# Scaling x by one bound per batch, and splitting and turning it by halves of the heads

## The chip, the core and the metric

The kernel runs on one core of one Trainium2 chip. The metric is the device time of one execution in microseconds; less is better. Before the change the median of three runs is 897.0 us (894.86, 897.0 and 897.5).

## What is computed

Attention in which a query sees only the keys of its own hash bucket, then a gated feed-forward layer ("MoE") on the result:

```python
q_bits = einsum('bhsd,dk->bhsk', q, proj) > 0      # 6 bits; k_bits likewise
mask = q_bucket[:, :, :, None] == k_bucket[:, :, None, :]
scores = where(mask, matmul(q, k.T) / sqrt(64), -1e9)
attn = softmax(scores)                             # sum + 1e-9
x = matmul(attn, v)                                # 4 batches, 8 heads, 768 tokens, 64
x = x.transpose(0, 2, 1, 3).reshape(3072, 512)
out = ((x @ w_a) * (x @ w_b)) @ w_out              # 512 -> 1536 -> 512
```

## The kernel before, in words

A *unit* is (b, c): one batch and 256 of its 768 tokens (b 0 to 3, c 0 to 2), 12 in all. It is handled in two *halves* of four heads, and a half is eight q-tiles of 128 queries by 768 keys. I call (b, c, half) a block.

For a q-tile TensorE makes the scores (L1053), VectorE the row maximum (L1067) and a width (L1076), ScalarE or VectorE a bias (L1083, L1089), and ScalarE the exponential with its row sum (L1099). The exponentials are split into a float16 hi part (L1110 to L1112) and the rest, lo (GpSimd L1122 or VectorE L1126), turned by a transposing DMA (L1132), and multiplied with the hi and lo parts of V in 18 matmuls (L1141, "av"). Unit (0,0) is done in float32 instead, and turned by TensorE (L1020, L1027, L1034). The products of a block collect in one PSUM tile `av`, of which there is one buffer.

V is loaded by pairs of heads; `vprep` (L765 on) takes a pair's largest value (`scale_pair`, L741 on: a reduction on ScalarE L751 or VectorE L754, then `scale_of`: a matmul, a maximum, three small instructions, L460 to L480), makes a power of two of it (`vsc`), and `veps`, a guard for the softmax sum (L780), and splits V into hi (L790, L794) and lo (L802). K and Q go through `split` (L883 to L904) and are turned by DMA, at the start by TensorE (L855) with an eviction (L863, L865).

`su_end` (L1149 on) closes a block. It makes r from the row sums (L1166, L1171, L1179), x = av * r (L1184), and for each token the sum of the absolute values of x (`sums`, L1195). After the second half `norm` (L1206 on) makes a power of two for each token with eight small instructions. Then x of the whole unit is scaled by it and split, one tile of 128 tokens after the other, into hi (L1237, L1241) and lo (L1248), each tile in two pieces, and each tile is turned by one DMA (L1260) into `xT`. In the first and the last unit x is scaled first (L1269), turned in float32 by TensorE (L1283) and split while it is evicted (L1295, L1298).

The MoE layer of a unit has 12 steps f. A step multiplies xT with two weights (L1346, 24 matmuls, tile `ab`), gates the two products (ScalarE L1360, VectorE L1368), splits the result (L1376 or L1380, GpSimd L1388), and multiplies with the output weight (L1398, tile `o`). At the end the scale is undone with `osc` (L1417), one column for each token tile, in the two evictions `ob` (L1428, L1434), and two DMAs store them (L1452). The tag `ob` has two buffers. The weights arrive as 64-bit numbers in the first quarter and are turned into hi and lo parts on all engines (L529 to L662).

The order of all work is fixed: each piece is an *entry* with a number, and the list `ORDER` names the entries in the order in which they are issued. Every engine runs its own entries in that order, and SP issues all DMAs in that order. Plus 10000 or 20000 picks an entry's first or second other engine. A negative number stands for that many filler matmuls on a dummy tile (`warm`, L1502). A tile takes a buffer of its tag when it is first written, and the buffer comes free when the last entry that uses the old tile is done.

Of the kernel before, what the change touches and what calls it, by code (L numbers as in the profile page):

```python
# [1540 lines left out]
```

## Time and profile before

| | |
|---|---|
| median of three runs | 897.0 us |
| profiled execution | 895.02 us, span 893.2 us |
| TensorE busy | 859.5 us, 9213 matmuls |
| VectorE busy | 649.4 us, 1561 instructions |
| ScalarE busy | 529.8 us |
| GpSimd busy | 450.8 us |
| TensorE's granted clock, mean | 0.998 |

The span runs from the first to the last instruction of the profiled execution. Busy times are of instructions at work; waiting for a semaphore is not busy. The filler matmuls count as busy TensorE time.

### The profile page before, as it was taken

To read this page: it belongs to the slowest core of one execution; us is meant where nothing else is said; L and a number is where in the kernel's file an instruction comes from. 1 tells how busy PE (TensorE), PEld (TensorE's weight loads), DVE (VectorE), ACT (ScalarE), POOL (GpSimd) and SP (SyncE) were. 2 spreads that over 40 slices of the span, in tenths; PEclk is the share of its full clock that TensorE was granted. 3 is DMA by queue.
4 is the path that set the end of the run, shared out by engine and by line. 5 is a ranking of instruction groups with operands and counts; after the bars stand their busy time and mean duration, and the time that the engine had idled before them with its cause. 6 is when DMAs were issued, how large, how long until landed. Compare 5 with 4: busy or idle time off the path is not lost.

```text
span 893.2 us, 23061 instructions
## 1 busy us (share of the span) xinstructions
PE 859.5 (96%) x9213; PEld 655.1 (73%) x9213; DVE 649.4 (73%) x1561; ACT 529.8 (59%) x1031; POOL 450.8 (50%) x396
## 2 busy tenths in 40 slices
PE   5789899999999999999999999999999999999998
PEld 4567777767777767777777777777777777777775
DVE  6899999888878968777875468777888865562210
ACT  7789999865654655566634466545675645442212
POOL 2578887663456465565153364554444455361111
PEclk9999999999999999999999999999999999999999
DMA  9986899999999999999977779997999957644000
GB/s 325 308 185 199 152 257 201 175 166 174 179 197 176 161 195 187 192 175 176 172 136 112 119 159 157 181 180 142 162 188 160 175 108 121 114 95 72 2 24 25
DMA packets 416988, 142.61 MB, mean 160 GB/s; under 512 B 388592, under 2 KB 409200, under 8 KB 416880
## 3 DMA queue, kind: packets, MB, share of 16 engines
q1 hardware_dynamic: 416880, 141.14, 82.4%
q8 instruction: 72, 1.18, 0.6%
q14 instruction: 36, 0.29, 0.1%
HBM read 37.82 MB, written 6.29 MB: 49 GB/s over the span
## 4 chain that ended last, share of the span: by engine, by line
PE 70%; DVE 6%; ACT 2%; DMA 2%; issue 1%; POOL 0%; ACTq 0%; SPq 0%; DVEq 0%
PE ab L1346 35%; PE o L1398 17%; PE s L1053 9%; PE av L1141 8%; DMA at<-a 2%; DVE mx L1067 1%; ACT e L1099 1%; DVE g L1368 1%; DVE xz L1248 1%; ACT a L1111 0%; DMA xT<-xz 0%; DVE a L1126 0%; DVE x L1184 0%; PE b_k L816 0%; PE b_q L816 0%
## 5 line engine op out<-in xcount | busy, mean ns | idle before, releaser
L1346 PE MATMUL ab<-xT,wab 128*128 128x256 f16 x3456 | 409.0, 273 | 2.2 <-DVE g L1368 1.9
L1346 PEld LDWEIGHTS <-wab 128*128 128x128 f16 x3456 | 332.3, 98 | 56.6 <-issue 4.1
L1122 POOL TENSOR_TENSOR a<-e,a 128x768 f16<-128x768 f32 x128 | 215.6, 1687 | 106.0 <-ACT a L1111 55.9
L1388 POOL TENSOR_TENSOR g<-g,g 128x256 f16<-128x256 f32 x144 | 106.2, 738 | 241.8 <-ACT g L1376 165.3
L1099 ACT ACTIVATE e<-s,bias,width 128x768 f32<-128x768 f32 x192 | 189.7, 988 | 62.3 <-DVE bias L1089 48.7
L1067 DVE TENSOR_REDUCE mx<-s 128x1 f32<-128x768 f32 x192 | 182.2, 951 | 43.7 <-PE s L1053 42.6
L1398 PE MATMUL o<-wo,g 128*128 128x512 f16 x864 | 208.3, 379 | 0.0
L1360 ACT ACTIVATE a<-ab,wcut 128x256 f32<-128x256 f32 x144 | 67.6, 469 | 136.8 <-PE ab L1346 135.7
L1368 DVE SCALAR_TENSOR_TENSOR g<-ab,wlow,a 128x256 f32<-128x256 f32 x132 | 63.5, 481 | 109.4 <-ACT a L1360 101.2
L1398 PEld LDWEIGHTS <-g 128*128 128x128 f16 x864 | 81.8, 98 | 75.9 <-issue 0.2
L1141 PEld LDWEIGHTS <-at 128*128 128x128 f16 x3168 | 112.3, 98 | 20.7 <-DMA at<-a 3.6
L1141 PE MATMUL av<-vh,at 128*128 128x64 f16 x2112 | 115.6, 193 | 2.3 <-DMA at<-a 1.7
L1053 PE MATMUL s<-kTA_k,qTA_q 128*128 128x384 f16 x384 | 94.5, 328 | 5.6 <-ACT e L1099 3.9
L1053 PE MATMUL s<-kTB_k,qTB_q 128*128 128x384 f16 x384 | 94.5, 328 | 0.0
L1112 POOL CAST a<-e 128x768 f16<-128x768 f32 x62 | 55.1, 893 | 41.5 <-ACT e L1099 31.5
L1083 ACT ACTIVATE bias<-mx,width 128x1 f32<-128x1 f32 x89 | 25.9, 293 | 73.0 <-DVE width L1076 72.9
L1111 ACT CAST a<-e 128x768 f16<-128x768 f32 x77 | 63.7, 829 | 7.8 <-DMA at<-a 6.7
L1376 ACT CAST g<-g 128x256 f16<-128x256 f32 x98 | 39.3, 401 | 44.7 <-DVE g L1368 37.5
L1141 PE MATMUL av<-vl,at 128*128 128x64 f16 x1056 | 59.6, 193 | 0.0
L1053 PEld LDWEIGHTS <-qTB_q 128*128 128x128 f16 x384 | 37.7, 98 | 25.3 <-issue 0.7
L1126 DVE TENSOR_TENSOR a<-e,a 128x768 f16<-128x768 f32 x48 | 47.4, 991 | 8.4 <-ACT a L1111 8.0
L1053 PEld LDWEIGHTS <-qTA_q 128*128 128x128 f16 x384 | 34.7, 99 | 22.5 <-issue 7.9
(156 smaller groups left out, 857.3 us busy)
## 6 DMA issues: line engine op xcount, KB each, us to landing
rk_k<-in_k_dram SPq DMA_DIRECT2D x16, 384.0 KB, 4.2
vr<-in_v_dram SPq DMA_DIRECT2D x16, 384.0 KB, 3.9
rq_q<-in_q_dram SPq DMA_DIRECT2D x12, 512.0 KB, 5.0
raw_w<-in_moe_w_b_dram SPq DMA_DIRECT2D x12, 512.0 KB, 7.6
raw_w<-in_moe_w_a_dram SPq DMA_DIRECT2D x12, 512.0 KB, 6.7
raw_wo<-in_moe_w_out_dram SPq DMA_DIRECT2D x12, 512.0 KB, 5.1
out_dram<-ob SPq DMA_DIRECT2D x24, 256.0 KB, 2.6
at<-a SPq DMA_TRANSPOSE x176, 4.1
```

Of the source, the lines that this page charges most:

```text
L1053: nc.tensor.matmul(ps.t[:, jj, :HALF], lhsT=x.t[:, uq, :], rhs=y.t[:, h * NT + jj * 3 : h * NT + jj * 3 + 3, :].rearrange("p t x -> p (t x)"),
L1067: lambda: nc.vector.tensor_reduce(out=mx.t[:, u : u + 1], in_=halves(ps.t), axis=AX.XY, op=ALU.max, negate=True),
L1099: lambda: nc.scalar.activation(flat2(e.t), halves(ps.t), AF.Exp, bias=bias.t[:, u : u + 1], scale=width.t[:, u : u + 1], accum_out=sm.t[:, ...
L1111: ("ACT", 0.725, lambda: nc.scalar.copy(out=a2.t[:, 0], in_=e.t), False),
L1112: ("POOL", 0.9, lambda: nc.gpsimd.tensor_copy(out=a2.t[:, 0], in_=e.t), False),
L1122: lambda: nc.gpsimd.tensor_tensor(out=a2.t[:, 1], in0=e.t, in1=a2.t[:, 0], op=ALU.subtract),
L1141: nc.tensor.matmul(av.t[:, u, :], lhsT=at.t[:, a + kt, :], rhs=w.t[:, h, kt, :], start=i == 0, stop=i == 3 * NT - 1,)
L1346: nc.tensor.matmul(pl.t[:, m, :CH], lhsT=wt(m, wi, cc, f), rhs=xt.t[:, :, xi * NC + cc, :], start=i == 0, stop=i == 3 * NC - 1,)
L1360: lambda a=a, pl=pl, gr=gr: nc.scalar.activation(a.t, pl.t[:, 0, :CH], AF.Copy, scale=wcut[:, gr : gr + 1]),
L1368: lambda a=a, g32=g32, pl=pl, cut=cut: nc.vector.scalar_tensor_tensor(out=g32.t, in0=pl.t[:, 1, :CH], scalar=cut, in1=a.t, op0=ALU.mult, o ...
L1388: lambda g=g, g32=g32: nc.gpsimd.tensor_tensor(out=g[1].t, in0=g32.t, in1=g[0].t, op=ALU.subtract),
L1398: nc.tensor.matmul(po.t[:, u, :], lhsT=g[gi].t[:, us], rhs=wo[f // 2].t[:, f % 2, wi * DM : (wi + 1) * DM], start=f % per_q == 0 and i == ...
```

## The change

- x is no longer scaled by its tokens. `x_scale` takes the smallest of a batch's four V scales; all rows of x of the batch are scaled by it through r, since hi and lo parts of V already carry their own scales. `sums`, `norm`, `veps` and the scaling in the first and last unit go away; the guard's factors come from `x_scale` too. `osc` becomes one column.
- So x of a half can be split and turned by itself: hi is one copy of 512 columns (ScalarE, VectorE or GpSimd), lo one subtraction (VectorE or GpSimd), and one DMA turns a half. The last and first unit turn four blocks a half on TensorE. x and its split tile z have one buffer each.
- r may be made by VectorE; the hi parts of k, q and v may be made by GpSimd; V's and K's reductions may all go to ScalarE.
- A batch's four V pairs stand ahead of its first block, since `x_scale` needs all four.
- `ORDER` is a new list: 3612 entries for 3658, 161 filler matmuls for 147. The arithmetic of the attention and of the MoE layer is the same otherwise.

The diff, cut; of the order only the parts that the prediction speaks of. Entry 27 loads the second key pair, 28 reduces it, 52 evicts qTA and 81 is x_scale of the first batch (the numbers 27, 28 and 52 are the same in both lists). At the end, before: 3654 and 3656 are the evictions of unit (3,2), 3655 and 3657 their stores. After: 3608 and 3610 the evictions, 3609 and 3611 the stores, 3352 the store of half 0 of unit (3,1).

```diff
...
 ORDER = [
-    13, 2, 1, 0, 53, 41, 61, 277, 276, 280, 10014, 8, 281, 9, 3, 258, 10, 5, 7, 15, -8, 11, 27, 150, 16, 6, 4, 10054,
...
-    287, 68, 289, 49, -4, 50, 294, 291, 51, -10, 10028, 296, 52, 256, 326, 10272, 323, 255, 322, 10139, 259, 10267,
...
+    4, 5, 13, 60, 0, 2, 1, 74, 41, 53, 67, 275, 10014, 271, 276, 10061, 248, 10003, 15, 272, 16, 8, 17, 252, 9, 62,
+    -8, 10, 249, 10075, 20018, 63, 11, 253, 64, 27, 6, 76, -16, 153, 20, 42, 77, 20065, 78, 10054, 43, 7, 12, 44, 55,
...
+    274, 25, 279, 71, 280, -9, 26, 45, 281, 250, 282, 10290, 81, 284, 49, -5, 50, 10262, 289, 254, 51, -9, 251, 10028,
+    255, 286, 52, 256, 291, 317, 257, -3, 318, 72, 29, 83, 30, 322, 258, 10154, 31, 91, 386, 259, 321, 20032, 84, 261,
...
-    3636, 3639, 3637, 3647, 3641, 3642, 3643, 3646, 3644, 3638, 3648, 3649, 3645, 3650, 3651, 3652, 3654, 3656, 3655,
-    3657,
+    3599, 3604, 3605, 3606, 3608, 3609, 13610, 3611, 3352,
...
+    def x_scale(b, key):
...
+        def go():
+            least, inv = xinv[:, b, 0:1], xinv[:, b, 1:2]
+            nc.vector.tensor_reduce(out=least, in_=vsc[:, own], axis=AX.X, op=ALU.min)
+            nc.vector.tensor_scalar(out=least, in0=least, scalar1=XTOP, scalar2=None, op0=ALU.min)
+            nc.vector.reciprocal(out=inv, in_=least)
...
+            nc.vector.tensor_scalar(out=least, in0=inv, scalar1=inv, scalar2=None, op0=ALU.mult)
...
-        op(
-            "DVE", 0.6,
-            lambda: nc.vector.tensor_reduce(
-                out=sums.t[:, :, half], in_=x.t.rearrange("p (j t h) d -> p t j (h d)", j=2, t=TPC), axis=AX.XY,
-                op=ALU.add, apply_absolute_value=True,
-            ),
-            key, r=[x], w=[(sums, half)],
-        )
...
+        if b * NCH + c not in X_BY_PE:
+            z = buf("z", [P, 2, 2 * TPC, P], F16, f"z_{n}", 1)
...
+            op(
+                "ACT", 0.51, lambda: nc.scalar.copy(out=part(0), in_=flat()), key, r=[x], w=[(z, "hi")], hold=[xt],
...
+            op(
+                "DVE", 0.61,
+                lambda: nc.vector.tensor_tensor(out=part(1), in0=flat(), in1=part(0), op=ALU.subtract),
+                key, r=[x, (z, "hi")], w=[(z, "lo")], sbuf=True,
...
-        op("DVE", 1.32, norm, key, r=[(sums, 0), (sums, 1)], w=[sc, sq])
...
-                                pl.t[:, m, :CH], lhsT=wt(m, wi, cc, f), rhs=xt.t[:, :, xi * NC + cc, :],
+                                pl.t[:, m, :CH], lhsT=wt(m, wi, cc, f), rhs=xt.t[:, cc // 2, xi, cc % 2 * TPC : (cc % 2 + 1) * TPC, :],
...
-            if i < 2:
-                for hp in (2 * half, 2 * half + 1):
...
+            if i == 0:
+                for hp in range(NPAIR):
...
+                x_scale(b, start)
```

## Rows read from the trace of the kernel before

**Rows 1.** The page's part 1: busy us, share of the span, instructions.
```profile
PE 859.5 (96%) x9213; PEld 655.1 (73%) x9213; DVE 649.4 (73%) x1561; ACT 529.8 (59%) x1031; POOL 450.8 (50%) x396
```
**Rows 2.** Busy time by stretches; the last three columns: clock, DMA share, GB/s.
```profile
0.00:30.00 30.00, 17.59 (x167) 12.48 (x168) 19.95 (x61) 21.00 (x25) 9.14 (x16) 0.94 0.94 345
30.00:108.00 78.00, 67.30 (x653) 55.92 (x651) 76.05 (x189) 70.41 (x116) 60.73 (x40) 1.00 0.78 192
108.00:200.00 92.00, 90.32 (x1004) 67.64 (x1003) 84.80 (x217) 80.55 (x145) 66.10 (x48) 1.00 1.06 201
200.00:800.00 600.00, 595.44 (x6623) 451.99 (x6621) 448.40 (x1050) 333.81 (x696) 297.24 (x270) 1.00 0.91 160
800.00:888.90 88.90, 88.85 (x775) 67.08 (x773) 20.23 (x47) 22.77 (x51) 17.55 (x24) 1.00 0.13 25
888.90:893.20 4.30, 0.00 (x0) 0.00 (x0) 0.00 (x0) 1.25 (x2) 0.00 (x0) 0.96 0.32 122
```
**Rows 3.** Groups of instructions: the filler (count, busy us, mean ns, idle before).
```profile
L1502 PE MATMUL warm<-ident 128*128 128x256 f16 x147 | 21.6, 288 | 0.0
```
**Rows 4.** TensorE's waits: us in total, times, longest.
```profile
PE s L1053 <- ACT e L1099: 3.9, 7, 0.9
...
PE ab L1346 <- DVE g L1368: 1.9, 3, 0.8
```
**Rows 5.** Groups of instructions on VectorE: count, busy us, mean ns, idle before.
```profile
L1248 DVE SCALAR_TENSOR_TENSOR xz<-x,xsc,xz 128x256 f16<-128x256 f32 x40 | 24.4, 654 | 0.0
...
L1089 DVE TENSOR_SCALAR bias<-mx,width 128x1 f32<-128x1 f32 x103 | 21.6, 211 | 2.3
...
L1184 DVE TENSOR_TENSOR x<-av,r 128x512 f32<-128x512 f32 x24 | 16.4, 684 | 3.5 <-PE av L1141 3.5
L1195 DVE TENSOR_REDUCE sums<-x 128x2 f32<-128x512 f32 x24 | 16.3, 680 | 0.3
...
L1210 DVE TENSOR_SCALAR xsq<-sums 128x1 f32<-128x1 f32 x24 | 4.9, 206 | 0.2
...
L1215 DVE TENSOR_SCALAR xsq<-xsq 128x1 int32<-128x1 int32 x24 | 3.7, 154 | 0.8
...
L780 DVE TENSOR_SCALAR veps<-vsc 128x1 f32<-128x1 f32 x16 | 2.3, 146 | 0.1
```
**Rows 6.** Timeline of ScalarE, then of TensorE, from 20 to 27 us.
```profile
20.44 0.83 ACT L751 ACTIVATE nB_k<-rk_k 128x768 bf16<-128x768 f32 x1
21.18 0.19 ACT L751 ACTIVATION_READ_ACCUMULATOR nB_k<-rk_k 128x1 f32 x1
21.27 1.84 ACT L863 COPY qTA_q<-t_q_ACT 128x2048 f16<-128x2048 f16 x1
25.11 0.84 ACT L751 ACTIVATE nB_k<-rk_k 128x768 bf16<-128x768 f32 x1 [2.00 <-DMA rk_k<-in_k_dram]
...
26.10 0.29 PE L460 MATMUL ps_k<-ident,mx_k 128*128 128x128 bf16 x1 [0.85 <-ACT nB_k L751]
26.18 0.84 PE L1053 MATMUL s<-kTA_k,qTA_q 128*128 128x384 f16 x2
```
**Rows 7.** The chain that ended last, late in the span: start, us, what.
```profile
784.87 0.53 PE av L1141 x18
785.40 2.62 PE ab L1346 x24
```
**Rows 8.** The tile x: one line's durations, ns min/median/max, first and last start.
```profile
L1248 DVE SCALAR_TENSOR_TENSOR xz<-x,xsc,xz x40: 470/479/1872, 167.5 to 761.1; 128x256 f16<-128x256 f32 x40
```
**Rows 9.** The tail: timelines of ScalarE and SP, landing of stores, VectorE's eviction.
```profile
888.89 1.26 ACT L1428 ACTIVATE ob<-o,osc 128x512 f32<-128x512 f32 x2 [2.27 <-PE o L1398]
...
889.60 0.91 SPq L1452 DMA_DIRECT2D out_dram<-ob  x2
...
DMA to landing us min/median/max: 2.0/2.6/4.6
...
L1434 DVE TENSOR_SCALAR ob<-o,osc 128x512 f32<-128x512 f32 x11 | 8.1, 746 | 2.0 <-ACT ob L1428 1.9 <-PE o L1398 0.2
```
**Rows 10.** Groups of instructions: the maximum in scale_of, for V.
```profile
L466 DVE TENSOR_REDUCE al_v<-ps_v 128x1 f32<-128x128 f32 x16 | 4.5, 282 | 2.3 <-PE ps_v L460 2.2
```

More of the change, by code (lines that the diff above doesn't have):

```diff
@@ L420, in attention_moe @@
     vsc = cp.tile([P, NB * NPAIR], F32, tag="vsc", name="vsc")
-    veps = cp.tile([P, NB * NPAIR], F32, tag="veps", name="veps")
+    xrel = cp.tile([P, NB, 2, NPAIR + 1], F32, tag="xrel", name="xrel")
+    xinv = cp.tile([P, NB, 2], F32, tag="xinv", name="xinv")
     wcut = cp.tile([P, NG], F32, tag="wcut", name="wcut")
@@ L631, in load_group, with most @@
                 cc = 2 * i + h
-                op(
-                    "DVE", 0.6,
-                    lambda raw=raw, cc=cc, h=h: nc.vector.tensor_reduce(
+                def most(eng, raw=raw, cc=cc, h=h):
+                    eng.tensor_reduce(
                         out=wmx[:, g, cc + 1 : cc + 2],
@@ L637, in load_group @@
                         apply_absolute_value=True,
-                    ),
-                    key + i + 0.5 * h, r=[(raw, "raw", h), "wmx"], w=[(mx, cc)],
+                    )
+                op(
+                    "DVE", 0.6, lambda most=most: most(nc.vector), key + i + 0.5 * h, r=[(raw, "raw", h), "wmx"],
+                    w=[(mx, cc)],
                 )
@@ L751, in total, with most @@
             nc.scalar.activation(junk(), flat(), AF.Abs, accum_out=mx.t)
-        def most():
-            nc.vector.tensor_reduce(
+        def most(eng=nc.vector):
+            eng.tensor_reduce(
                 out=mx.t, in_=t.t.rearrange("p h t d -> p (h t d)"), axis=AX.X, op=ALU.max,
@@ L777, in vprep @@
         )
-        op(
-            "DVE", 0.15,
-            lambda: nc.vector.tensor_scalar(
-                out=veps[:, col : col + 1], in0=sc, scalar1=ESC * 1e-9, scalar2=None, op0=ALU.mult
-            ),
-            key + 4, r=[("v1", col)], w=[("vsc", col)],
-        )
         def flat(x):
@@ L797, in vprep, with low @@
                 True,
-            )],
-        )
-        op(
-            "DVE", 1.0,
-            lambda: nc.vector.scalar_tensor_tensor(
-                out=flat(vl), in0=flat(vr), scalar=sc, in1=flat(vh), op0=ALU.mult, op1=ALU.subtract
-            ),
-            key_b, r=[vr, ("v1", col), vh], w=[vl], sbuf=True,
+            ), (
+                "POOL", 0.85,
+                lambda: nc.gpsimd.tensor_scalar(
+                    out=flat(vh), in0=flat(vr), scalar1=sc, scalar2=None, op0=ALU.mult
+                ),
+                False,
+            )],
+        )
+        def low(eng):
+            eng.scalar_tensor_tensor(
+                out=flat(vl), in0=flat(vr), scalar=sc, in1=flat(vh), op0=ALU.mult, op1=ALU.subtract
+            )
+        op(
+            "DVE", 1.0, lambda: low(nc.vector), key_b, r=[vr, ("v1", col), vh], w=[vl], sbuf=True,
+        )
+    def x_scale(b, key):
+        own = slice(b * NPAIR, (b + 1) * NPAIR)
+        def go():
[3 more added lines that the diff above has]
+            nc.vector.reciprocal(out=inv, in_=least)
+            nc.vector.tensor_scalar(
+                out=xrel[:, b, 0, :NPAIR], in0=vsc[:, own], scalar1=inv, scalar2=None, op0=ALU.mult
+            )
+            nc.vector.tensor_scalar(
+                out=xrel[:, b, 1, :NPAIR], in0=vsc[:, own], scalar1=inv, scalar2=ESC * 1e-9, op0=ALU.mult, op1=ALU.mult
+            )
+            if b == 0:
+                nc.vector.tensor_copy(out=xrel[:, b, 0, NPAIR:], in_=inv)
+                nc.vector.tensor_scalar(out=xrel[:, b, 1, NPAIR:], in0=inv, scalar1=1e-9, scalar2=None, op0=ALU.mult)
+            nc.vector.tensor_scalar(out=least, in0=inv, scalar1=inv, scalar2=None, op0=ALU.mult)
+        op(
+            "DVE", 0.61 if b else 0.81, go, key, r=[("v1", b * NPAIR + hp) for hp in range(NPAIR)],
+            w=[("xsc", b)],
         )
@@ L890, in split @@
                 True,
+            ), (
+                "POOL", 0.1 + 0.065 * n,
+                lambda: nc.gpsimd.tensor_scalar(
+                    out=part(B, hi_at), in0=x, scalar1=sc.t, scalar2=None, op0=ALU.mult
+                ),
+                False,
             )],
@@ L901, in split, with low @@
         )
-        op(
-            "DVE", -0.03 + 0.073 * n,
-            lambda: nc.vector.scalar_tensor_tensor(
-                out=part(B, lo_at), in0=x, scalar=sc.t, in1=part(B, hi_at), op0=ALU.mult, op1=ALU.subtract
-            ),
-            key, r=[raw, *rtoks, (B, "hi")], w=[(B, "lo")], sbuf=True,
+        def low(eng):
+            eng.scalar_tensor_tensor(
+                out=part(B, lo_at), in0=x, scalar=sc.t, in1=part(B, hi_at), op0=ALU.mult, op1=ALU.subtract
+            )
+        op(
+            "DVE", -0.03 + 0.073 * n, lambda: low(nc.vector), key, r=[raw, *rtoks, (B, "hi")], w=[(B, "lo")],
+            sbuf=True,
         )
@@ L1061, in qtile @@
         )
-        whole = (b, c) in F32_UNITS
+        whole = (b, c, half) in F32_UNITS
         top = 0.0 if whole else LN_ESC
@@ L1161, in su_end, with columns, guarded, guarded_too @@
         us = range(4 * TPC)
-        col = b * NPAIR + 2 * half
-        def guarded():
-            if (b, c) in F32_UNITS:
-                nc.scalar.activation(r.t, sm.t, AF.Copy, scale=1.0, bias=1e-9)
-                return
+        def columns():
+            whole = (b, c, half) in F32_UNITS
             for j in range(2):
                 js = slice(2 * TPC * j, 2 * TPC * (j + 1))
-                at = col + j
-                nc.scalar.activation(
-                    r.t[:, js], sm.t[:, js], AF.Identity, scale=vsc[:, at : at + 1], bias=veps[:, at : at + 1]
-                )
-        op(
-            "ACT", 0.56, guarded, key, r=[(sm, u) for u in us] + ([] if (b, c) in F32_UNITS else [("vsc", col), ("vsc", col + 1)]),
-            w=[r],
+                at = NPAIR if whole else 2 * half + j
+                yield js, xrel[:, b, 0, at : at + 1], xrel[:, b, 1, at : at + 1]
+        def guarded():
+            for js, y, z in columns():
+                nc.scalar.activation(r.t[:, js], sm.t[:, js], AF.Identity, scale=y, bias=z)
+        def guarded_too():
+            for js, y, z in columns():
+                nc.vector.tensor_scalar(
+                    out=r.t[:, js], in0=sm.t[:, js], scalar1=y, scalar2=z, op0=ALU.mult, op1=ALU.add
+                )
+        op(
+            "ACT", 0.56, guarded, key, r=[(sm, u) for u in us] + [("xsc", b)],
+            w=[r], alt=[("DVE", 0.24, guarded_too, False)],
         )
         op("DVE", 0.13, lambda: nc.vector.reciprocal(out=r.t, in_=r.t), key, r=[r], w=[r])
-        x = buf("x", [P, 4 * TPC, D], F32, f"x_{n}")
-        xx.append(x)
+        x = buf("x", [P, 4 * TPC, D], F32, f"x_{n}", 1)
         op(
@@ L1204, in su_end @@
-        sq = tsq[b, c] = buf("x_sq", [P, TPC], F32, f"xsq_{b}_{c}", 3)
-        def norm():
-            for t in range(TPC):
-                y = sq.t[:, t : t + 1]
-                z = sc.t[:, t : t + 1]
-                nc.vector.tensor_scalar(
-                    out=y, in0=sums.t[:, t, 0:1], scalar1=sums.t[:, t, 1:2], scalar2=float(2.0**-46),
-                    op0=ALU.add, op1=ALU.max,
-                )
-                y, z = y.bitcast(I32), z.bitcast(I32)
-                nc.vector.tensor_scalar(out=y, in0=y, scalar1=0x7F800000, scalar2=None, op0=ALU.bitwise_and)
-                nc.vector.tensor_scalar(
-                    out=z, in0=y, scalar1=-1.0, scalar2=float(268 << 23), op0=ALU.mult, op1=ALU.add
-                )
-                nc.vector.tensor_scalar(
-                    out=y, in0=y, scalar1=float(-155 << 22), scalar2=2.0, op0=ALU.add, op1=ALU.mult
-                )
@@ L1266, in su_end @@
-        for i, y in enumerate(xx):
-            def scaled(eng, y=y):
-                eng.tensor_tensor(
-                    out=by_tile(y), in0=by_tile(y),
-                    in1=sc.t.unsqueeze(1).unsqueeze(3).to_broadcast([P, 2, TPC, 2 * D]), op=ALU.mult,
-                )
-            op(
-                "POOL", 1.25, lambda scaled=scaled: scaled(nc.gpsimd), key, r=[y, sc], w=[(y, "norm")],
-                alt=[("DVE", 0.62, lambda scaled=scaled: scaled(nc.vector), True)],
-            )
+        xt = xT[b, c]
@@ new lines, in flat, with side, part @@
+        def flat():
+            return x.t.rearrange("p u d -> p (u d)")
+        def side(i):
+            return xt.t[:, half, i].rearrange("p u x -> p (u x)")
+        if b * NCH + c not in X_BY_PE:
+            z = buf("z", [P, 2, 2 * TPC, P], F16, f"z_{n}", 1)
+            def part(i):
+                return z.t[:, i].rearrange("p u x -> p (u x)")
+            op(
+                "ACT", 0.51, lambda: nc.scalar.copy(out=part(0), in_=flat()), key, r=[x], w=[(z, "hi")], hold=[xt],
+                alt=[
+                    ("DVE", 0.34, lambda: nc.vector.tensor_copy(out=part(0), in_=flat()), True),
+                    ("POOL", 0.56, lambda: nc.gpsimd.tensor_copy(out=part(0), in_=flat()), False),
+                ],
+            )
+            op(
+                "DVE", 0.61,
+                lambda: nc.vector.tensor_tensor(out=part(1), in0=flat(), in1=part(0), op=ALU.subtract),
+                key, r=[x, (z, "hi")], w=[(z, "lo")], sbuf=True,
+                alt=[(
+                    "POOL", 1.1,
+                    lambda: nc.gpsimd.tensor_tensor(out=part(1), in0=flat(), in1=part(0), op=ALU.subtract), False,
+                )],
+            )
+            op(
+                "SP", T_ISSUE * 8 / 12,
+                lambda: nc.sync.dma_start_transpose(
+                    out=xt.t[:, half].rearrange("p i u x -> p (i u) x"), in_=z.t.rearrange("p i u x -> p (i u x)")
+                ),
+                key, r=[(z, "hi"), (z, "lo")], w=[(xt, half)], svc=2.2 * 8 / 12,
+            )
+            return
@@ L1278, in su_end @@
         ps = psum(f"px_{n}", tag)
         def tps():
-            for h, y in enumerate(xx):
-                for u in range(2 * TPC):
-                    nc.tensor.transpose(
-                        out=ps.t[:, h, u * P : (u + 1) * P],
-                        in_=y.t[:, 2 * u : 2 * u + 2, :].rearrange("p h d -> p (h d)"), identity=ident,
-                    )
-        def side(i):
-            return xt.t[:, :, i * NC : (i + 1) * NC, :].rearrange("p t c x -> p c t x")
-        def both():
-            return ps.t.rearrange("p h (j t x) -> p (h j) t x", j=2, t=TPC)
@@ L1294, in su_end @@
-        op("PE", 0.9, tps, key, r=[(y, "norm") for y in xx] + ["ident"], w=[ps], hold=[xt])
-        op("ACT", 0.9, lambda: nc.scalar.copy(out=side(0), in_=both()), key, r=[ps], w=[(xt, "hi")])
-        op(
-            "DVE", 1.2,
-            lambda: nc.vector.tensor_tensor(out=side(1), in0=both(), in1=side(0), op=ALU.subtract),
-            key, r=[ps, (xt, "hi")], w=[(xt, 0), (xt, 1)],
+            for u in range(2 * TPC):
+                nc.tensor.transpose(
+                    out=ps.t[:, 0, u * P : (u + 1) * P],
+                    in_=x.t[:, 2 * u : 2 * u + 2, :].rearrange("p h d -> p (h d)"), identity=ident,
+                )
@@ new lines, in su_end @@
+        op("PE", 0.45, tps, key, r=[x, "ident"], w=[ps], hold=[xt])
+        op(
+            "ACT", 0.52, lambda: nc.scalar.copy(out=side(0), in_=ps.t[:, 0]), key, r=[ps], w=[(xt, half, "hi")],
+            alt=[("DVE", 0.62, lambda: nc.vector.tensor_copy(out=side(0), in_=ps.t[:, 0]), False)],
+        )
+        op(
+            "DVE", 0.63,
+            lambda: nc.vector.tensor_tensor(out=side(1), in0=ps.t[:, 0], in1=side(0), op=ALU.subtract),
+            key, r=[ps, (xt, half, "hi")], w=[(xt, half)],
@@ L1323, in moe @@
         xt = xT[b, c]
-        xtok = [(xt, t) for t in range(TPC)]
-        sq = tsq[b, c]
+        xtok = [(xt, half) for half in range(2)]
         ob = [buf("ob", [P, DM], F32, f"ob_{b}_{c}_{u}") for u in range(TPC)]
@@ L1412, in moe @@
             ke = kf + lag
-            osc = buf("osc", [P, TPC], F32, f"osc_{n}", 3)
+            osc = buf("osc", [P, 1], F32, f"osc_{n}", 3)
             op(
-                "DVE", 0.24,
-                lambda total=total, osc=osc: [
-                    nc.vector.tensor_scalar(
-                        out=osc.t[:, u : u + 1], in0=sq.t[:, u : u + 1], scalar1=total, scalar2=None, op0=ALU.mult
-                    )
-                    for u in range(TPC)
-                ],
-                ke - 8, r=[sq, "wtop" if whole else ("wall", fq)], w=[osc],
+                "DVE", 0.12,
+                lambda total=total, osc=osc: nc.vector.tensor_scalar(
+                    out=osc.t, in0=xinv[:, b, 0:1], scalar1=total, scalar2=None, op0=ALU.mult
+                ),
+                ke - 8, r=[("xsc", b), "wtop" if whole else ("wall", fq)], w=[osc],
             )
```

66 lines of the change are left out of this document (10 added, 56 removed), and 373 rows, old and new, of the table ORDER.

## The prediction

> **What bounds the kernel now.** I read the busy totals first, to see which engine is full: TensorE is busy for 859.5 of 893.2 us, VectorE for 649.4 [rows 1]. A share that high leaves only TensorE's idle time to win, so the table by stretches comes next [rows 2]. From 200 to 800 us TensorE is busy 595.44 of 600 and VectorE only 448.40: work taken from VectorE there is worth nothing by itself. The other side of the table is the front. Up to 108 us, where the first MoE matmul starts, TensorE is idle for 12.41 + 10.70 = 23.1 us, and part of what counts as busy is filler: 147 dummy matmuls, 21.6 us [rows 3]. So about 44.7 us of the front are not useful TensorE time. Between 30 and 108 us VectorE is busy 76.05 of 78 (97.5%) and ScalarE 70.41 (90%): that stretch goes at VectorE's pace. The rest of the waste is 1.68 us (108 to 200), 4.56 us (200 to 800) and 4.3 us after the last matmul. Useful TensorE work is 893.2 - 44.7 - 10.6 = 837.9 us, and the change touches none of it: the same matmuls run, on another layout of x. The waits of TensorE [rows 4] say what ended its idle pieces: the exponential freeing a score buffer (3.9 us, mostly in the front) and the gate product on VectorE (1.9 us).
>
> So three places can move: the front, the few late waits, the tail.
>
> **What leaves VectorE.** 24 absolute sums at 0.680 (16.3 us), 96 small instructions of the per-token power of two (24 at 0.206 and 72 at 0.154, 16.0 us), 16 of veps (2.3 us) [rows 5]. Added: x_scale, 8 small instructions for the first batch and 6 for each later one, 26 at 0.154 = 4.0 us. The lo parts go from 40 at 0.654 to 20 of double length; the row of that length (x, 0.684, one operand in PSUM) prices them at 13.7 against 24.4 us. Together some 40 of 649 us leave. The hi parts on ScalarE are likewise halved in number, and 15 splits of k, q and v go to GpSimd with 17 pieces of x. Nine tenths of this lies after 108 us, beside TensorE at 99%, and is costed at nothing; the cover is the MoE matmul stream, and if that cover were gone it would be worth up to the 6.2 us of idle time there.
>
> **Front, start.** Today the reduction of the second key pair runs on ScalarE at 20.44, then the eviction of qTA until 23.1, and the first score follows at 26.18, behind the scale matmul of the third pair (26.10) [rows 6]. The new list loads all four V pairs ahead of the weights, and moves the second key pair (entry 27) from the 13th to the 18th transfer on SP's queue, behind all eight of the first weight transfers. Its reduction (10028) still stands ahead of the qTA eviction (52) on ScalarE. The nearest row for a key pair behind that much traffic is the third pair's today: reduced from 25.11. Then the eviction ends at 25.11 + 0.84 + 0.18 + 1.84 = 28.0, and the first score moves by about +1.7. Bound below: it lands as early as today, and the scores, now ahead of the third pair's matmul, start about 1.0 earlier. A fourth V reduction (1.0, the same form at 0.84 + 0.18) has by then been done early, so 0.7 of the 1.7 is lost. I take **+0.7** (-1.0 to +1.7).
>
> **Front, pace.** The two issue lists can be counted at the same point, the first score of block (0,2,0). Ahead of it VectorE has 231 entries for 234, ScalarE 136 for 134, GpSimd 58 for 65. VectorE's direct saving up to there is 2 sums, one norm (1.33) and 4 veps, 3.3 us, less x_scale 1.2 and two r pairs (4 at 0.211): 1.2 us; the other exchanges (products, casts taken over from GpSimd) spend it again. What is bought: TensorE has one more ab half (12 of the 24 in 2.62: 1.31) and one more av (0.53) in front [rows 7], 1.8 us of useful work for the same vector work. I take **-1.8**; bounds -0.6 (the exchanged entries cost another 1.2) and -2.6 (the 7 GpSimd entries fewer free VectorE as well).
>
> **Late waits.** Half of the 1.9 us that TensorE waits for the gate product: **-1.0**. Bounds: -2.9, half of all idle time after 108 us, and 0. Here a row speaks for caution: the lo pieces take 470 at least, 479 in the median and 1872 ns at most [rows 8], so now and then a two-operand instruction is held for about 1.4 us. The Trainium skill ("SBUF — State Buffer", section "Who interferes with whom") says that a VectorE instruction with two SBUF inputs and a GpSimd instruction that reads SBUF exclude each other for a whole instruction, whichever is second; what it would do to the sum is the last rival below.
>
> **Tail.** After the last matmul (888.86) ScalarE evicts both halves of the last unit's output, 1.26 us to 890.15, and SP issues the two stores [rows 9]. In the new list the end reads: evict half 0 (3608, ScalarE), store it (3609), evict half 1 (13610, VectorE), store it (3611), and last of all 3352, the store of the *previous* unit's half 0. The tag ob has two buffers. One still holds that previous half, since its store is behind everything on SP. So half 1 must take the buffer of half 0, after its store has landed. A store takes 2.0 at least and 2.6 us in the median to land. Issue 889.60, landed 891.6 to 892.2, eviction on VectorE 0.746: 892.35 to 892.95 instead of 890.15, +2.2 to +2.8; the third issue (0.91 / 2) adds up to 0.5. Nothing is left to hide this. I take **+2.5** (+2.2 to +3.3).
>
> **Sum.** +0.7 - 1.8 - 1.0 + 2.5 = +0.4. The profiled execution took 895.02 us (span 893.2), 2.0 below the median of the three runs; I add the sum to the median: 897.4 us. No change means within 0.3% (2.7 us), about what a measurement of this kernel can tell: 894.3 to 899.7.
>
> **Rivals.** *Relief pays (faster).* Start -0.5 (half its lower bound), pace -2.6, late waits -2.9, tail +2.2: -3.8, 893.6 us. For it: VectorE is what the front runs at; against: in 200 to 800 us TensorE already waits for only 0.8%. *The batch scale gates (slower).* x of the first block of a batch now needs the V scales of all four pairs. If the last V pair is reduced later than that block's last exponential, r and x wait for al (0.282 [rows 10]), three small instructions (0.46), x_scale (0.92) and the reduction itself (1.0): 2.7 us; x frees the single av bank, so the next av, and all TensorE work behind it in order, waits. In the new list x_scale stands 33, 11 and 15 entries ahead of r in batches 1 to 3; two tight ones make +5.4: 902.8 us. It decides as soon as TensorE's av of the second block is next in line. *The front pays nothing.* Start +1.7, tail +2.5: +4.2, 901.6 us. For it: the new list has 161 fillers, 72 of them ahead of the first score where 57 stood, so more idle time was planned there. *GpSimd blocks VectorE.* If each of the 8 new splits on GpSimd ahead of block (0,2,0) holds a VectorE instruction once for the 1.4 us by which the longest lo exceeds the median, that is 11.1 us of a 97.5% busy engine, 908.5 us. The page of the Trainium skill named above would have this happen whenever such a pair meets. The trace shows it as a rare case (the mean is 654, the median 479), and GpSimd has 7 entries fewer there. *The tail wait isn't there* (the buffers are handed out otherwise): 894.9 us, still no change.
>
> **Numbers.** Forecast with the tail rival 0.52, relief 0.25, batch scale 0.11, empty front 0.08, GpSimd 0.04. Faster is 0.25, same 0.52, slower 0.11 + 0.08 + 0.04 = 0.23. The range runs from the relief case to the empty front, 893.6 to 901.6; outside lie the two dear cases (0.15).
>
> **What would show it.** Right: about 40 us less VectorE and no fewer TensorE matmuls; the first score near 28; the first MoE matmul before 108; idle time from 200 to 800 us at or below 4.6; at the end two evictions more than 2 us apart with VectorE waiting for a store, and some 6.8 us from the last matmul to the end. Wrong: evictions side by side at the end, av waiting for x at a batch's start, VectorE's lo near 1.9 us as a rule, or an idle sum in the front that moves by more than 3 us.

## The result and the profile after

The changed kernel takes 906.32 us (median of 4 runs, 905.78 to 908.81) against 895.93 us before on the same chip: a ratio of 1.0119, 95% interval 1.0091 to 1.0146. It is slower by some 10 us, where I had forecast 897.4 us and a range up to 901.6. The profiled execution took 906.14 us with a span of 904.4, so the 11.2 us by which the span grew (893.2 before) is what has to be found.

Totals of the page after:

```profile
span 904.4 us, 22976 instructions
...
PE 863.4 (95%) x9227; PEld 655.3 (72%) x9227; DVE 649.8 (72%) x1474; ACT 502.2 (56%) x969; POOL 461.8 (51%) x389
```

VectorE was to lose 40 us and lost nothing (649.4 before). The table by stretches, with the columns of [rows 2]:

```profile
0.00:30.00 30.00, 18.33 (x191) 13.92 (x192) 22.57 (x76) 23.05 (x29) 14.56 (x16) 1.00 0.84 298
30.00:108.00 78.00, 67.14 (x599) 55.23 (x597) 72.76 (x164) 66.45 (x108) 57.21 (x32) 0.98 0.77 206
108.00:200.00 92.00, 87.82 (x1028) 65.96 (x1027) 85.85 (x210) 78.97 (x140) 67.11 (x49) 1.00 1.04 201
200.00:800.00 600.00, 592.92 (x6571) 447.45 (x6569) 441.61 (x976) 309.61 (x641) 301.20 (x268) 1.00 0.87 158
```

TensorE's work without fillers tells how far a kernel is. Up to 200 us it was 17.59 + 67.30 + 90.32 - 21.64 = 153.6 us before [rows 2, 3]. Now it is 18.33 + 67.14 + 87.82 = 173.29, less 161 fillers of 23.05 us in all: 150.2. So 3.4 us are lost by 200 us. From 200 to 800 another 592.92 against 595.44, 2.5 us, are lost. The last matmul ends at 897.23 instead of 888.86, 8.4 us late; the remaining 2.5 us of these stand in no idle time: the same 9066 matmuls besides the fillers keep TensorE busy for 840.3 us instead of 837.9. Part of that can be the lower clock (0.98 in the mean from 30 to 108 us, 1.00 before); how much is not shown. What follows the last matmul takes 904.4 - 897.23 = 7.2 us for 4.3.

What VectorE does instead (lines and engine groups, columns as in [rows 5]); first three groups of before that were not shown, then the same work after, and the new r:

```profile
L1126 DVE TENSOR_TENSOR a<-e,a 128x768 f16<-128x768 f32 x48 | 47.4, 991 | 8.4 <-ACT a L1111 8.0 <-POOL a L1112 0.3
...
L1110 DVE CAST a<-e 128x768 f16<-128x768 f32 x37 | 21.4, 577 | 13.0 <-ACT e L1099 10.9 <-issue 1.6 <-DMA at<-a 0.2
L1380 DVE TENSOR_REDUCE g<-g 128x256 f16<-128x256 f32 x46 | 19.1, 415 | 3.5 <-PE o L1398 2.6
```

```profile
L1164 DVE TENSOR_TENSOR a<-e,a 128x768 f16<-128x768 f32 x66 | 66.4, 1009 | 7.8 <-ACT a L1149 5.4 <-POOL a L1150 2.2
...
L1148 DVE CAST a<-e 128x768 f16<-128x768 f32 x58 | 34.7, 601 | 7.8 <-ACT e L1137 6.2 <-DMA at<-a 1.3
L1364 DVE TENSOR_REDUCE g<-g 128x256 f16<-128x256 f32 x69 | 28.6, 415 | 6.4 <-PE o L1382 4.6
L939 DVE SCALAR_TENSOR_TENSOR nB_k<-rk_k,ks_k,nB_k 128x768 f16<-128x768 f32 x16 | 20.1, 1255 | 4.8 <-POOL nB_k L923 3.7 <-ACT nB_k L913 0.9
...
L803 DVE SCALAR_TENSOR_TENSOR vl<-vr,vsc,vh 128x768 f16<-128x768 f32 x16 | 19.0, 1191 | 3.8 <-POOL vh L795 3.6
...
L1212 DVE TENSOR_SCALAR r<-sm,xrel 128x4 f32<-128x4 f32 x22 | 15.1, 731 | 0.0
```

The sums, the norm and veps are gone as forecast. In their place VectorE has 18 more lo parts of the softmax (47.4 to 66.4 us), 21 more casts (21.4 to 34.7), 23 more hi parts of the gate (19.1 to 28.6) and r, 15.1 us: 57 us. The 18 lo parts and nine of the casts were GpSimd's; 12 casts, the 23 gate parts and r were ScalarE's, whose busy time falls from 529.8 to 502.2. GpSimd has other work instead:

```profile
L1160 POOL TENSOR_TENSOR a<-e,a 128x768 f16<-128x768 f32 x110 | 189.2, 1723 | 81.7 <-DVE a L1148 49.5 <-ACT a L1149 20.4 <-issue 5.4
...
L1150 POOL CAST a<-e 128x768 f16<-128x768 f32 x53 | 49.2, 927 | 27.6 <-ACT e L1137 16.0 <-DMA at<-a 9.1 <-ACT a L1149 1.8
...
L795 POOL TENSOR_SCALAR vh<-vr,vsc 128x768 f16<-128x768 f32 x6 | 15.1, 2519 | 3.9 <-PE b_k L846 2.0 <-ACT vh L785 1.9
L923 POOL TENSOR_SCALAR nB_k<-rk_k,ks_k 128x768 f16<-128x768 f32 x6 | 14.6, 2426 | 12.9 <-DVE ks_k L480 7.8 <-DVE wsc L602 5.0
L1256 POOL TENSOR_TENSOR z<-x,z 128x512 f16<-128x512 f32 x12 | 13.8, 1154 | 1.8 <-ACT z L1244 1.8
...
L923 POOL TENSOR_SCALAR nB_q<-rq_q,qsc_q 128x1024 f16<-128x1024 f32 x3 | 9.4, 3144 | 1.1 <-ACT e L1137 1.1
```

A split of 768 columns takes GpSimd 2.4 to 2.5 us in the mean, where the list planned 0.85 to 0.88 and a plain cast of 768 columns takes 0.93. The lo parts on VectorE wait for them (3.7 and 3.6 us), mostly behind the front: up to 112 us the key parts wait 1.8 us for GpSimd, the query parts 0.8 and the V parts not at all.

And r: a timeline of VectorE and GpSimd at two of its 11 places (start, duration):

```profile
146.48 2.15 DVE L1212 TENSOR_SCALAR r<-sm,xrel 128x4 f32<-128x4 f32 x2
146.96 1.65 POOL L1160 TENSOR_TENSOR a<-e,a 128x768 f16<-128x768 f32 x1
...
747.06 0.47 DVE L1212 TENSOR_SCALAR r<-sm,xrel 128x4 f32<-128x4 f32 x2
```

The first pair ends at 148.63, as the GpSimd instruction does (148.61); the second meets none and takes 0.47 us.

The tail, as the timeline has it:

```profile
897.26 0.69 ACT L1409 ACTIVATE ob<-o,osc 128x512 f32<-128x512 f32 x1 [2.27 <-PE o L1382]
897.97 3.70 SPq L1433 DMA_DIRECT2D out_dram<-ob  x3
900.08 0.75 DVE L1415 TENSOR_SCALAR ob<-o,osc 128x512 f32<-128x512 f32 x1 [5.59 <-DMA out_dram<-ob]
```

The second eviction starts at 900.08, once a store has landed. So there are three suspects: the splits on GpSimd, r on VectorE, and the last entry of the list.

### The profile page after: what moved, and what is told of

Same layout as the page of the kernel before. It is cut to its first block, busy times and chain, and to the rows that moved or that the text cites. A ratio compares the mean times of both kernels' runs of the same rounds, so it can differ in the third digit from the quotient of the medians.

```text
span 904.4 us, 22976 instructions
## 1 busy us (share of the span) xinstructions
PE 863.4 (95%) x9227; PEld 655.3 (72%) x9227; DVE 649.8 (72%) x1474; ACT 502.2 (56%) x969; POOL 461.8 (51%) x389
## 4 chain that ended last, share of the span: by engine, by line
PE 67%; DVE 6%; DMA 6%; ACT 2%; POOL 2%; issue 2%; ACTq 0%; DVEq 0%; POOLq 0%
PE ab L1330 34%; PE o L1382 16%; PE s L1091 9%; PE av L1179 8%; DMA at<-a 4%; DVE mx L1105 1%; POOL a L1160 1%; ACT e L1137 1%; DVE r L1212 1%; DVE a L1164 1%; DMA rq_q<-in_q_dram 1%; DVE g L1352 1%; DMA xT<-z 0%; ACT a L1344 0%; ACT a L1149 0%
## 5 line engine op out<-in xcount | busy, mean ns | idle before, releaser
L1160 POOL TENSOR_TENSOR a<-e,a 128x768 f16<-128x768 f32 x110 | 189.2, 1723 | 81.7 <-DVE a L1148 49.5
L1164 DVE TENSOR_TENSOR a<-e,a 128x768 f16<-128x768 f32 x66 | 66.4, 1009 | 7.8 <-ACT a L1149 5.4
L1150 POOL CAST a<-e 128x768 f16<-128x768 f32 x53 | 49.2, 927 | 27.6 <-ACT e L1137 16.0
L1121 ACT ACTIVATE bias<-mx,width 128x1 f32<-128x1 f32 x98 | 28.2, 292 | 62.1 <-DVE width L1114 61.8
L1149 ACT CAST a<-e 128x768 f16<-128x768 f32 x65 | 53.5, 830 | 5.2 <-DMA at<-a 4.5
L1360 ACT CAST g<-g 128x256 f16<-128x256 f32 x75 | 30.1, 401 | 37.7 <-DVE g L1352 20.4
```

The costliest lines, as they stand in the source:

```text
L1149: ("ACT", 0.725, lambda: nc.scalar.copy(out=a2.t[:, 0], in_=e.t), False),
L1160: lambda: nc.gpsimd.tensor_tensor(out=a2.t[:, 1], in0=e.t, in1=a2.t[:, 0], op=ALU.subtract),
L1164: lambda: nc.vector.tensor_tensor(out=a2.t[:, 1], in0=e.t, in1=a2.t[:, 0], op=ALU.subtract), True,
```

## The experiments

All edits but three are in the list `ORDER` alone. The second other engine of a split is GpSimd, the first of r is VectorE.

**The 15 splits back on ScalarE.**

```diff
-20018, 20065, 20058, 20032, 20158, 20170, 20557, 20814, ...
+18, 65, 58, 32, 158, 170, 557, 814, ...
```

> The changed kernel with its 15 hi splits of k, q and v (nine k and q, six v) taken off GpSimd and put on ScalarE, at the same places of the list. Theory (GpSimd blocks VectorE): these splits take 2.2 to 2.9 us each on GpSimd in the changed kernel, and the lo parts on VectorE wait for them (4.8 us before the k parts, 3.6 us before the v parts) and are stretched by them; on ScalarE they take under 1 us, so the first MoE matmul comes 2 to 5 us earlier at equal useful TensorE work and the whole is 2 to 4 us shorter than the changed kernel's 906.3: 902 to 904. Rival (the front is bound by something else, ScalarE's 66 of 78 us being as full as VectorE): ScalarE's evictions and exponentials come later by what GpSimd gave it, within 1 us of 906.3.

Measured 901.25 us, ratio to before 1.0057 (1.0043 to 1.0072): 5 us shorter than the changed kernel, more than the 2 to 4 that the theory expected. From 30 to 108 us:

```profile
30.00:108.00 78.00, 68.17 (x636) 56.62 (x634) 73.89 (x173) 72.99 (x119) 44.20 (x27) 1.00 0.81 214
```

ScalarE rises from 66.45 to 72.99 us, and TensorE does 37 more matmuls there. Up to 200 us its work without fillers is 19.59 + 68.17 + 88.03 - 23.57 = 152.2 (150.2 in the changed kernel), and the clock is back at 1.00. The first MoE matmul starts at 102.7 us instead of 105.5. Two groups of the changed kernel, then of this run, up to 112 us:

```profile
L939 DVE SCALAR_TENSOR_TENSOR nB_k<-rk_k,ks_k,nB_k 128x768 f16<-128x768 f32 x4 | 6.5, 1619 | 1.8 <-POOL nB_k L923 1.8
...
L939 DVE SCALAR_TENSOR_TENSOR nB_q<-rq_q,qsc_q,nB_q 128x1024 f16<-128x1024 f32 x3 | 4.5, 1498 | 0.8 <-POOL nB_q L923 0.8
```

```profile
L939 DVE SCALAR_TENSOR_TENSOR nB_q<-rq_q,qsc_q,nB_q 128x1024 f16<-128x1024 f32 x3 | 5.0, 1659 | 0.3 <-ACT nB_q L913 0.3
L939 DVE SCALAR_TENSOR_TENSOR nB_k<-rk_k,ks_k,nB_k 128x768 f16<-128x768 f32 x4 | 4.7, 1174 | 1.6 <-ACT nB_k L913 1.5
```

So the lo parts of the front lose 1.3 us of length (11.0 to 9.7) and 0.7 of waiting (2.6 to 1.9). In the changed kernel TensorE's transposes also wait once, 1.4 us, for a key's lo part, and this run shows no such wait of a matmul. Through which waits the rest of the 5 us comes back is not shown.

**r back on ScalarE**, alone.

```diff
-10242, 10637, 10716, 11564, 11742, 11821, 12590, 13181, 13260, 13438, 13517
+242, 637, 716, 1564, 1742, 1821, 2590, 3181, 3260, 3438, 3517
```

> The changed kernel with its 11 pairs of r (the tiny scaling of the bound, 128x4) taken off VectorE and put back on ScalarE, at the same places. Theory: on VectorE these 22 instructions took 16.1 us, up to 1.7 us for four columns, each ending as a GpSimd instruction ends; on ScalarE a pair takes about 0.8, so VectorE loses some 16 us and ScalarE gains 8. If x on VectorE is what the next av waits for, the whole is 1 to 3 us shorter: 903 to 905.5. Rival: 9 of the 11 lie after 108 us, where TensorE is busy 99%, so nothing: 905.5 to 907.

Measured 904.93 us, ratio 1.0099 (1.0072 to 1.0126). The single times spread from 900.3 to 908.4 us, and the interval overlaps that of the changed kernel: this run does not settle it.

**The last store moved up.**

```diff
-3351, ... 3608, 3609, 13610, 3611, 3352,
+3351, 3352, ... 3608, 3609, 13610, 3611,
```

> The changed kernel with one entry moved: the store of half 0 of the last but one unit goes from the last place of the list to just behind its eviction. Theory (the tail as forecast): the last unit's second eviction no longer waits for a store, the stretch from the last matmul to the end falls from 7.2 to about 4.3 us, nothing else moves: 2.5 to 3.0 us shorter, 903.4. Rival: the second eviction waits for something else (the store of the unit's own first half is on the way anyway), under 1 us.

Measured 902.99 us, ratio 1.0078 (1.0058 to 1.0099): 3.3 us shorter. This interval just overlaps that of the changed kernel as well; here the trace decides. What follows the last matmul takes 4.4 us instead of 7.2, the evictions start 0.7 us apart, and SP issues two stores:

```profile
895.81 0.69 ACT L1409 ACTIVATE ob<-o,osc 128x512 f32<-128x512 f32 x1 [2.27 <-PE o L1382]
896.52 1.12 SPq L1433 DMA_DIRECT2D out_dram<-ob  x2
896.53 0.75 DVE L1415 TENSOR_SCALAR ob<-o,osc 128x512 f32<-128x512 f32 x1 [3.49 <-ACT ob L1409]
```

**All three.**

> The changed kernel with all three edits: hi splits and r on ScalarE, the store moved. Theory: the parts add, 906.3 - 2.9 (tail) - 3 (splits) - 2 (r) = 898.4, between 897 and 900.5: then still no faster than the kernel before (895.9). Rival (ScalarE becomes the bound when it gets both): only the tail's 2.9 us, 903.4.

Measured 896.34 us over 12 runs, ratio 0.9998 (0.9985 to 1.0011): better than expected and equal to before. The three edits bring the whole 10 us back, and alone they give 5.1 + 1.4 + 3.3 = 9.8. Its totals, and its stretches:

```profile
PE 862.0 (96%) x9227; PEld 656.9 (73%) x9227; DVE 633.2 (71%) x1452; ACT 520.1 (58%) x1006; POOL 424.3 (47%) x374
```

```profile
30.00:108.00 78.00, 68.10 (x635) 56.73 (x633) 72.80 (x170) 73.30 (x119) 44.80 (x28) 1.00 0.79 209
...
200.00:800.00 600.00, 594.61 (x6582) 450.44 (x6580) 431.63 (x958) 319.77 (x663) 286.40 (x262) 1.00 0.87 158
```

VectorE is now 16 us lighter than before, and the time is the same: the relief buys nothing that can be measured here.

**The kernel before with its store moved last**, the counterpart of the tail.

```diff
-3396, ... 3654, 3656, 3655, 3657,
+... 3654, 3656, 3655, 3657, 3396,
```

> The kernel before with one entry moved: the store of half 0 of the last but one unit goes to the last place of the list, as in the changed kernel. Theory (buffer of the output and SP's order, as forecast): VectorE or ScalarE's second eviction waits for a store, 2.2 to 3.3 us longer than the kernel before. Rival (the changed kernel's tail is long for another reason, such as the eviction on VectorE): within 1 us.

Measured 899.05 us against 896.29, ratio 1.0032 (1.0016 to 1.0047), +2.8 us. Here ScalarE does both evictions, and the second waits just so; the rival falls:

```profile
889.58 0.69 ACT L1428 ACTIVATE ob<-o,osc 128x512 f32<-128x512 f32 x1 [2.27 <-PE o L1398]
890.29 3.61 SPq L1452 DMA_DIRECT2D out_dram<-ob  x3
892.38 0.69 ACT L1428 ACTIVATE ob<-o,osc 128x512 f32<-128x512 f32 x1 [2.12 <-DMA out_dram<-ob]
```

**The kernel before with eight splits on GpSimd.** GpSimd's form of the instruction was added as an alternative in `split` and `vprep`, and eight entries of batch 0 use it.

```diff
+            ), ("POOL", 0.1 + 0.065 * n, lambda: nc.gpsimd.tensor_scalar(
+                out=part(B, hi_at), in0=x, scalar1=sc.t, scalar2=None, op0=ALU.mult), False)],
```

> The kernel before with eight hi splits of the first batch moved from ScalarE to GpSimd at their own places of the list: the four key pairs, V pairs 0 and 1, query blocks 1 and 2. Theory (a GpSimd split of 2.2 to 2.8 us in place of ScalarE's 0.9 delays the lo parts on VectorE and the transposes behind it): 3 to 6 us longer than before. Rival (the cost lies in the changed kernel's list, not in the splits; ScalarE at 90% is glad of the relief): within 1.5 us, or faster.

Measured 905.22 us, ratio 1.0103 (1.0082 to 1.0125): +8.9 us, more than the theory's 6. The stretch from 30 to 108 us, then GpSimd and TensorE at the longest wait for GpSimd, and the same transposes in the kernel before:

```profile
30.00:108.00 78.00, 66.48 (x553) 56.08 (x551) 70.36 (x172) 59.29 (x99) 62.45 (x38) 0.91 0.71 187
```

```profile
14.27 4.39 POOL L798 TENSOR_SCALAR vh<-vr,vsc 128x768 f16<-128x768 f32 x2
...
18.61 0.82 POOL L895 COPY marked<-nB_k 128x768 f16<-128x768 f16 x1
...
19.49 1.46 PE L855 MATMUL t_k_ACT<-ident,marked 128*128 128x128 f16 x12 [4.45 <-POOL marked L895]
```

```profile
15.99 0.83 PE L855 MATMUL t_k_ACT<-ident,marked 128*128 128x128 f16 x12 [0.72 <-DVE marked L829]
```

The first key pair's hi part is copied by GpSimd into the other operand (`marked`, L895). In this list that copy stands behind two V splits in GpSimd's order, and TensorE's transposes wait 4.4 us for it. The first score comes at 29.39 us instead of 26.18, and the first MoE matmul at 117.7 instead of 108.1. The changed kernel has no such delay (first score at 26.45). So this run shows that splits on GpSimd are dear in another list too; it does not measure what they cost in the changed one.

TensorE's granted clock was 0.91 in the mean from 30 to 108 us, against 1.00 before. Right behind the wait, from 19.4 to 24.0 us, it was 0.50, the lower level of 1.2 GHz (1.00 before): the twelve transposes took 1.46 us instead of 0.83. So what TensorE did do took longer as well.

**Only the late splits on GpSimd.** All three edits, except that the seven splits of batches 1 to 3 stay where the change put them.

> As the kernel with all three edits (896.3), but the seven hi splits of batches 1 to 3 stay on GpSimd, so that only the eight of the first batch are on ScalarE. Theory (only the front, where VectorE and ScalarE are over 90% busy, pays for a split; behind 108 us TensorE's work covers it): within 1 us of 896.3. Rival (each split costs the same wherever it stands, 5.0 / 15 = 0.34 each): 898.7.

Measured 896.74 us, ratio 1.0005 (0.9992 to 1.0018): +0.4. The rival's 898.7 would be a ratio of 1.0027, outside the interval. The theory holds: what the splits cost, the eight of the first batch cost.

**r on VectorE again**, with the two other edits kept.

> As the kernel with all three edits (896.3), but the 11 pairs of r stay on VectorE: r alone told apart, since the run that moved r alone left it at -1.4 with an interval of the same size. Theory (r on VectorE is held behind GpSimd instructions, in front of the x that frees the av bank): 1 to 2.5 us longer, 897.5 to 899. Rival (r is hidden everywhere): within 0.7 us.

Measured 898.8 us, ratio 1.0026 (1.0015 to 1.0038), +2.5 us against the run with all three edits, whose interval ends at 1.0011. So r on VectorE does cost something, which the run with r alone had left open. The kernels also form a chain of one edit each: 906.3 (changed), 901.25 (splits back), 898.8 (store moved), 896.34 (r back).

Where r costs it, the two traces only indicate. From 108 to 200 us TensorE is busy for 86.99 us with r on VectorE and for 89.11 with all three edits; from 200 to 800 us it is 594.62 and 594.61. Only three of the 11 places lie before 200 us (92.7, 112.3 and 144.0). But the run with the splits back, which is the same kernel up to the last stores, has 88.03 in the first of these stretches, so single executions differ by about as much.

**The split by a constant**, to measure the form alone.

```diff
-                    out=part(B, hi_at), in0=x, scalar1=sc.t, scalar2=None, op0=ALU.mult
+                    out=part(B, hi_at), in0=x, scalar1=1.0, scalar2=None, op0=ALU.mult
```

> The changed kernel, in which the hi splits on GpSimd multiply by the constant 1.0 in place of the scale read from a column of SBUF (this leaves the scale out of those 15 hi parts). It measures the form alone. Theory (the scale read per partition makes the form slow): the 768-column splits fall from 2.20 us to about 0.85, like a plain cast of that size in the changed kernel (0.93 in the mean), and the whole comes near the run with the splits on ScalarE, 901 to 903. Rival (an f32 operand through GpSimd's arithmetic, or the shared port, sets the time): they stay at 2.0 us or more.

A single execution took 903.5 us, which says little of the whole; these splits also need not wait for their scale. My theory falls, the rival holds: 2.13 us at least for 768 columns with a constant (2.20 with a scale from SBUF).

```profile
L923 POOL TENSOR_SCALAR nB_k<-rk_k x6: 2127/2227/2835, 4.8 to 215.3; 128x768 f16<-128x768 f32 x6
L923 POOL TENSOR_SCALAR nB_q<-rq_q x3: 2765/2768/2770, 55.5 to 432.0; 128x1024 f16<-128x1024 f32 x3
```

This form of instruction is slow there with or without the scale from SBUF. The three query splits took 2.77 us each, nearly without spread, so 2.8 us for 1024 columns is the instruction's own time, not a hold.

**Four weight casts from ScalarE to GpSimd**, on top of all three edits, to see whether ScalarE had become the bound.

```diff
-264, ... 269, ... 331, ... 403,
+20264, ... 20269, ... 10331, ... 20403,
```

> As the kernel with all three edits (896.3), with four weight casts of the front (three hi parts of 1.04 us and one int32 piece of 1.15 us) moved from ScalarE, which is over 90% busy there, to GpSimd, which sits idle for 12 us around 65 us. Plain casts cost GpSimd no more than ScalarE. Theory (ScalarE now bounds the front): 1 to 3 us shorter, 893.5 to 895.5, then faster than the kernel before. Rival (VectorE, at 9.9 of 10 in the same slices, bounds it as well, or the casts wait in GpSimd's order): within 1 us of 896.3 or longer.

Measured 896.98 us, ratio 1.0003 (0.9993 to 1.0013). ScalarE falls to 68.98 us from 30 to 108 us (73.30), VectorE is at 71.72 (72.80), the granted clock at 0.96 (1.00), and nothing is gained: the rival holds. Which half of it holds, VectorE or GpSimd's order, is not told apart.

**r in one-column instructions.**

```diff
-                nc.vector.tensor_scalar(
-                    out=r.t[:, js], in0=sm.t[:, js], scalar1=y, scalar2=z, op0=ALU.mult, op1=ALU.add
-                )
+                for u in range(js.start, js.stop):
+                    nc.vector.tensor_scalar(out=r.t[:, u : u + 1], in0=sm.t[:, u : u + 1],
+                        scalar1=y, scalar2=z, op0=ALU.mult, op1=ALU.add)
```

> As the kernel with r on VectorE and the two other edits (898.8), but each r is made by eight one-column instructions in place of two of four columns. Theory (the instruction of four columns claims something that GpSimd's running instruction holds; one of a single column does not, as none of the 286 one-column scalings of the changed kernel took more than 0.22 us): 88 instructions of 0.2 us, none over 0.25, where the four-column ones took 0.28 to 1.71; the whole 0 to 2 us shorter, 896.5 to 899. Rival (r is held by something that it waits for, whatever its form): the first of each eight still takes up to 1.7 us.

The instruction (min/median/max in ns), first in four columns, from the run with r on VectorE again, then in one:

```profile
L1212 DVE TENSOR_SCALAR r<-sm,xrel x22: 277/681/1707, 92.7 to 823.6; 128x4 f32<-128x4 f32 x22
```

```profile
L1213 DVE TENSOR_SCALAR r<-sm,xrel x88: 259/264/273, 93.0 to 826.5; 128x1 f32<-128x1 f32 x88
```

None is held any more: a hold belongs to the four-column form, not to something that r waits for. But one takes 0.26 us, not 0.2, and the whole takes 900.92 us, ratio 1.0047 (1.0029 to 1.0065), not less as I had expected. The 88 instructions keep VectorE busy for 16.9 us where 22 of four columns took 16.4. So taking the holds away gives nothing back. That r costs by VectorE's time, about 1.5 us at each of its 11 places, held or not, fits both runs but is not shown.

## Why the prediction was wrong

Put together, in medians: 906.3 is 895.9 plus the splits (+5.1), the tail (+2.4 in the chain, +2.8 in the kernel before, 3.3 back in the changed one) and r (+2.5): 10.0 to 10.4 with the first two sizes of the tail. The rest of the change comes to zero, as the run with all three edits shows.

The range itself has a slip. The cases "relief pays" (-3.8) and "the front pays nothing" (+4.2) are whole sums, yet I added them to the forecast, which already has +0.4, and not to 897.0. The range should have been 893.2 to 901.2. The measured time lies outside either.

- **Tail, +2.5: right.** What follows the last matmul took 7.2 us, forecast 6.8; the buffer and the order of the stores were read rightly from the list, and the one-entry edit costs +2.8 in one kernel and gives 3.3 in the other.
- **The 15 splits: the step that failed most.** I let them "go to GpSimd" within a paragraph that put nine tenths behind 108 us and costed them at nothing; the sum has no term for them. Of the splits that was not so: eight of the 15 stand in front, as my own rival of GpSimd counted. Nor did I bound the price of an operation that the trace of before does not show on that engine. GpSimd's nearest rows were its two-operand subtraction of the same 768 columns and its cast, and ScalarE's price for the split was 0.93 us:

```profile
L1122 POOL TENSOR_TENSOR a<-e,a 128x768 f16<-128x768 f32 x128 | 215.6, 1687 | 106.0 <-ACT a L1111 55.9 <-DVE a L1110 36.8 <-issue 7.0
...
L1112 POOL CAST a<-e 128x768 f16<-128x768 f32 x62 | 55.1, 893 | 41.5 <-ACT e L1099 31.5 <-DMA at<-a 9.3 <-PE av L1034 0.6
...
L883 ACT ACTIVATE nB_k<-rk_k,ks_k 128x768 f16<-128x768 f32 x11 | 10.2, 931 | 3.9 <-DVE ks_k L480 3.8
```

  An estimate from these rows: eight splits at the upper one, 0.76 us dearer each, are some 6 us in a stretch where the others are 90 to 97% busy. The splits of 768 columns took 2.2 us at least and 2.4 to 2.5 in the mean, and the 15 cost 5.1 us: next to nothing for the seven behind 108 us (+0.4), the rest for the eight in front.
- **"GpSimd blocks VectorE", 908.5 us with a chance of 0.04:** near by its number, and it named the right eight entries, but that it came so near is luck. I had them hold VectorE for 11.1 us in all. Up to 112 us the lo parts of K and Q are 1.3 us longer with the splits on GpSimd, and those of V not at all. What the traces do show is that the splits are long, and that work stands behind them in order: a lo part and its transpose in the changed kernel, the copy and its transpose in the kernel before with eight splits.
- **r at 0.211: mis-sized, and mostly left out.** The row I took it from has one column. With four the mean is 0.73 us, up to 1.7. The sum has two of the 11 pairs, and the account of what leaves VectorE has none of them. On VectorE r cost +2.5 us. Why four columns are held is not shown by a run, but the hold shown ends with GpSimd's instruction. Here the page of the Trainium skill that I had set against the lo parts, "SBUF — State Buffer", section "Who interferes with whom", bears on it: a VectorE scaling that enters a two-port mode and a GpSimd instruction lock each other out for a whole instruction. The pair that ends 0.02 us behind GpSimd's and the one-column form that is never held agree with it; in which mode r ran no run here shows.
- **VectorE, -40 us: wrong.** What the diff removes is gone, 34.6 us of it. But the list is part of the change: it hands VectorE 18 lo parts, 21 casts, 23 gate parts and r, 57 us, from GpSimd and ScalarE. I had counted the lists up to one score near the front, and not by kind over the whole.
- **Pace, -1.8, and late waits, -1.0: wrong in sign.** The first MoE matmul does come earlier (105.5 us), as I had set for a sign of it, yet with less work done: 3.4 us less by 200 us. A first matmul moves with the order; the sum of useful work does not. Idle time from 200 to 800 us is 7.1, not below 4.6. With all three edits the work by 200 us is 19.76 + 68.10 + 89.11 - 23.60 = 153.4, as before (153.6), and idle time is 5.4: the relief that I priced at -2.8 is worth nothing. Of the other rivals, "the batch scale gates" has no sign: TensorE's av waits for x once, for 0.5 us, in the unit done in float32.
- **Start, +0.7:** the first score came at 26.45 (26.18 before), inside the bounds, but not near the 28 that I had set for a sign.

## What to carry to other kernels

Before work is moved to an engine, find that very form on that engine in a trace, operation, type and width, or bound it by the slowest neighbour: a price in the planner's table is a wish. When an order is searched anew, count the instructions of each kind on each engine over the whole list, since what is removed from one engine may be filled up with another's work. And read the last entries of a list against its buffers: one store in the last place cost 2.8 us.
